# Talking-heads attention and FFN: scores per head with full-height query blocks, moved by SBUF-to-SBUF DMA into tiles of 10 queries x 12 heads for head mixing; q and k transposed by DMA

## The chip, the cores and the metric

The kernel runs on one core of one Trainium2 chip. The metric is the device time of one execution, in microseconds; the text gives medians. Before the change it was 792.39 us (3 runs, 792.29 to 793.1).

## The reference

Eight batches, 12 heads, 448 positions, head dimension 64; inputs and output are float32. The heads are mixed twice, by two 12 x 12 matrices, before and after the softmax. Then comes a feed-forward layer (FFN) with squared ReLU.

```python
# q, k, v: (8, 12, 448, 64); w_pre, w_post: (12, 12)
scores = scale * np.matmul(q, k.transpose(0, 1, 3, 2))
scores = np.einsum('bhij,hg->bgij', scores, w_pre)       # mix heads
attn = softmax(scores)                                    # over j
attn = np.einsum('bhij,hg->bgij', attn, w_post)          # mix heads
out = np.matmul(attn, v)                                  # -> x, (3584, 768)
h = np.maximum(x @ w_in, 0.0)                             # w_in: (768, 2048)
return h * h @ w_out                                      # w_out: (2048, 768)
```

## The kernel before

TensorE works in the program's order. All other engines' instructions are ordered by a scheduler when the kernel is built. Each engine then runs its own queue strictly in order; the timelines below show VectorE doing so, with 10.4 us idle before one copy and ready work behind it.

To mix heads, heads must lie on partitions. The kernel before gets this from score matmuls of 32 columns: 16 queries of two heads at a time, four row and column tiles of the array in parallel. Twelve heads x 16 queries are 192 rows, so that two chunks of 16 queries fill three tiles of 128 partitions, and the mixing matmuls need several matrices (`preA`, `preBA`, `preBB`) and two passes. q and k are transposed by TensorE, as units of the batch before.

```python
    def transposes(ps, tiles, p):                 # q and k: TensorE, 4 per pair of heads
        for st in range(4):
            n = ROWS[st]
            nc.tensor.transpose(ps[:, 128 * st:128 * st + n],
                                tiles[st][0:n, 2 * p:2 * p + 2, :].rearrange("s h d -> s (h d)"), ident[0:n, 0:n])

    def k_unit(b, p):
        ps = bank("kt_ps", BF16)
        transposes(ps, staged[b][1], p)
        ...
        nc.scalar.copy(out=kt_p[:, :], in_=ps[:, 0:S])
        ...
    # ... (q_unit: the same, evacuated by VectorE)

    def score_tile(s, t):
        b, c = s
        ps = bank("s_ps")
        for r in range(4):
            p, n = (r, 2 * c + t) if t < 2 else (4 + r % 2, 2 * c + r // 2)
            nc.tensor.matmul(ps[32 * r:32 * r + 32, 0:S], lhsT=ql[b % 2][p][:, n, :], rhs=kts[(b, p)][:, :],
                             start=True, stop=True)
        ...

    def mix_O(s, u):
        ps = bank("m_ps")
        nc.tensor.matmul(ps[:, 0:S], lhsT=preA[:, 0:128], rhs=S_sb[(s, u)][:, :], start=True, stop=False)
        nc.tensor.matmul(ps[:, 0:S], lhsT=preBA[u][:, :], rhs=S_sb[(s, 2)][:, :], start=False, stop=True)
        softmax_tile(s, ps, u)
    # ... (mix_AB, mix_BB: the third tile; post, post_last: the second mixing)
```

The softmax here doesn't subtract the row's maximum and nothing guards it: scores larger than these inputs give would overflow.

## Time and profile before

| | before |
|---|---|
| time, median | 792.39 us |
| TensorE (PE) busy | 750.2 us, 95% |
| VectorE (DVE) / ScalarE (ACT) busy | 62% / 61% |
| first mixing matmul at | 27.9 us |
| start to start of the batches | 67.5 us (no FFN in it), then 93 to 95, the last 84.1 |
| after the last mixing matmul | 48.5 us |

The batch times are read from the starts of the mixing matmuls in the trace. The head of the profile page shows the busy time of each engine with its share and number of instructions; a row of 40 digits shows the granted TensorE clock in tenths (9 is full speed); the queue lines give packets, MB and the share of the 16 DMA engines' time; the chain is the work that ended last, by engine.

```profile
span 791.2 us, 18851 instructions
PE 750.2 (95%) x7586; PEld 428.6 (54%) x7586; DVE 488.6 (62%) x1249; ACT 482.3 (61%) x1337; POOL 243.2 (31%) x271
...
PEclk9999999999999999999999999999999999999999
...
q0 software_dynamic: 140032, 23.60, 39.0%
q1 hardware_dynamic: 8704, 11.03, 4.2%
...
PE 85%; DVE 11%; DMA 2%; ACT 1%; issue 1%; ACTq 0%; DVEq 0%
```

TensorE is the limit: it is busy nearly all the time, at full clock, and 85% of the chain lies on it. The list of waits (what waited <- what released it: us in total, times, longest) shows that it hardly waits:

```profile
PE at_ps L359 <- DVE d_sb L315: 20.3, 29, 3.4
PE kt_ps L180 <- DMA kst<-in_k_dram: 10.1, 4, 6.0
```

### The profile page before, as it was taken

The numbers are of one execution on the slowest core, as the hardware profiler recorded it, in microseconds if no ns is written. First come the engines' busy times: TensorE is split into PE (matmuls) and PEld (weight loads), VectorE is DVE, ScalarE is ACT, GpSimd is POOL, SyncE is SP. The second block draws the span as 40 slices with busy tenths as digits, with TensorE's granted clock in tenths as the row PEclk, the third lists the DMA queues.
The fourth block names the chain that finished last, engine by engine and source line by source line (L and its number), as shares of the span: only waits on it lengthen the run. The fifth ranks groups of instructions, "written<-read, shape, count | busy, mean of one in ns | idle before, by whom it ended". The sixth has DMA issues, their size and how long they took to land.

```text
span 791.2 us, 18851 instructions
## 1 busy us (share of the span) xinstructions
PE 750.2 (95%) x7586; PEld 428.6 (54%) x7586; DVE 488.6 (62%) x1249; ACT 482.3 (61%) x1337; POOL 243.2 (31%) x271
## 2 busy tenths in 40 slices
PE   3689899999999999999999999999999999999997
PEld 1245455555555555556555555555555565555654
DVE  2889868557685577656676576855766556555500
ACT  1477767547664577556766466754776457664641
POOL 6835255200570023700445005620053000420070
PEclk9999999999999999999999999999999999999999
DMA  9999967310690124911637106731060010001002
GB/s 111 74 206 158 66 41 51 42 46 7 41 72 31 41 16 28 70 42 31 41 25 57 51 12 41 50 42 46 7 42 1 32 41 2 2 12 50 12 1 70
DMA packets 149336, 35.85 MB, mean 45 GB/s; under 512 B 139264, under 2 KB 148480, under 8 KB 149248
## 3 DMA queue, kind: packets, MB, share of 16 engines
q0 software_dynamic: 140032, 23.60, 39.0%
q1 hardware_dynamic: 8704, 11.03, 4.2%
q8 instruction: 59, 0.97, 0.5%
q14 instruction: 29, 0.24, 0.1%
q10 hardware_dynamic: 512, 0.01, 0.1%
HBM read 47.21 MB, written 11.01 MB: 74 GB/s over the span
## 4 chain that ended last, share of the span: by engine, by line
PE 85%; DVE 11%; DMA 2%; ACT 1%; issue 1%; ACTq 0%; DVEq 0%
PE o_ps L263 19%; PE h_ps L245 18%; PE s_ps L291 8%; PE m_ps L327 6%; PE at_ps L345 6%; DVE d_sb L315 6%; PE at_ps L348 5%; PE m_ps L328 5%; PE mB_ps L321 4%; PE ot_ps L223 4%; DVE at L350 3%; PE mB_ps L305 2%; PE qt_ps L180 2%; PE kt_ps L180 2%; PE at_ps L359 2%; DMA postB_col<-in_w_post_dram 1%
## 5 line engine op out<-in xcount | busy, mean ns | idle before, releaser
L350 DVE CAST at<-at_ps 128x384 bf16<-128x384 f32 x336 | 184.0, 552 | 93.3 <-PE at_ps L348 90.4
L315 DVE TENSOR_SCALAR d_sb<-e_sb,rc 128x448 bf16<-128x448 f32 x336 | 171.9, 514 | 7.6
L295 ACT CAST s_sb<-s_ps 128x448 bf16<-128x448 f32 x224 | 108.2, 535 | 54.7 <-PE s_ps L291 52.8
L311 ACT ACTIVATE e_sb<-m_ps 128x448 f32<-128x448 f32 x224 | 121.1, 545 | 27.8 <-issue 23.9
L249 ACT ACTIVATE hr<-h_ps 128x448 f32<-128x448 f32 x128 | 69.7, 544 | 84.8 <-PE h_ps L245 84.0
L313 DVE RECIPROCAL rc<-sm 128x1 f32<-128x1 f32 x336 | 53.6, 160 | 100.5 <-ACT e_sb L311 99.6
L348 PE MATMUL at_ps<-postA,d_sb 128*128 128x192 bf16 x672 | 110.3, 246 | 0.0
L345 PE MATMUL at_ps<-postBB,d_sb 128*128 128x384 bf16 x336 | 109.9, 327 | 0.0
L297 DVE CAST s_sb<-s_ps 128x448 bf16<-128x448 f32 x112 | 69.8, 623 | 40.9 <-PE s_ps L291 40.9
L348 PEld LDWEIGHTS <-d_sb 128*128 128x128 bf16 x672 | 65.7, 98 | 40.8 <-issue 0.2
L327 PE MATMUL m_ps<-s_sb,preA 128*128 128x448 bf16 x224 | 80.3, 358 | 0.0
L269 ACT COPY osb<-o_ps 128x384 f32<-128x384 f32 x56 | 26.8, 479 | 71.4 <-PE o_ps L263 61.0
L311 ACT ACTIVATE e_sb<-mB_ps 128x448 f32<-128x448 f32 x112 | 63.1, 563 | 8.4 <-PE mB_ps L321 6.6
L359 PE MATMUL at_ps<-postA,d_sb 128*32 128x192 bf16 x448 | 37.3, 249 | 20.9 <-DVE d_sb L315 20.3
L82 POOL DMA_DIRECT2D v_0_79<-in_v_dram x4 | 4.3, 1066 | 152.0 <-PE ot_ps L230 151.2
L71 POOL DMA_DIRECT2D kst<-in_k_dram x32 | 32.1, 1012 | 51.9 <-PE kt_ps L180 43.6
L236 ACT ACTIVATE xt<-ot_ps,bvec 128x224 bf16<-128x224 f32 x96 | 37.7, 444 | 14.6 <-PE ot_ps L230 13.9
L311 ACT ACTIVATION_READ_ACCUMULATOR e_sb<-m_ps 128x1 f32 x224 | 46.1, 206 | 0.0
L245 PE MATMUL h_ps<-xt,w_0_191 128*128 128x448 bf16 x128 | 45.1, 353 | 0.0
L245 PE MATMUL h_ps<-xt,w_5_196 128*128 128x448 bf16 x128 | 45.1, 353 | 0.0
L245 PE MATMUL h_ps<-xt,w_2_193 128*128 128x448 bf16 x128 | 45.1, 352 | 0.0
L245 PE MATMUL h_ps<-xt,w_3_194 128*128 128x448 bf16 x128 | 45.1, 352 | 0.0
(602 smaller groups left out, 1921.4 us busy)
## 6 DMA issues: line engine op xcount, KB each, us to landing
out_dram<-osb SPq DMA_DIRECT2D x48, 192.0 KB, 1.9
kst<-in_k_dram POOLq DMA_DIRECT2D x24, 192.0 KB, 5.2
qst<-in_q_dram POOLq DMA_DIRECT2D x24, 192.0 KB, 5.0
out_dram<-osb SPq DMA_DIRECT2D x16, 96.0 KB, 2.2
kst<-in_k_dram POOLq DMA_DIRECT2D x8, 96.0 KB, 4.6
qst<-in_q_dram POOLq DMA_DIRECT2D x8, 96.0 KB, 3.9
v_0_76<-in_v_dram POOLq DMA_DIRECT2D x4, 192.0 KB, 4.7
v_1_77<-in_v_dram POOLq DMA_DIRECT2D x4, 192.0 KB, 6.0
```

The source lines that it names most:

```text
L245: nc.tensor.matmul(ps[:, 0:S], lhsT=w1[c2][:, ft * 128:(ft + 1) * 128], rhs=xts[(b, c2)][:, :], start=(c2 == 0), stop=(c2 == NPAIR - 1))
L249: nc.scalar.activation(out=hr[:, :], in_=ps[:, 0:S], func=ACT.Relu)
L263: nc.tensor.matmul(dst, lhsT=h2ts[(b, ft)][:, mt * 128:mt * 128 + ROWS[mt]], rhs=w2[ft][:, n2 * 384:(n2 + 1) * 384], start=(ft == 0), stop ...
L291: nc.tensor.matmul(ps[32 * r:32 * r + 32, 0:S], lhsT=ql[b % 2][p][:, n, :], rhs=kts[(b, p)][:, :], start=True, stop=True)
L295: nc.scalar.copy(out=sb[:, :], in_=ps[:, 0:S])
L297: nc.vector.tensor_copy(out=sb[:, :], in_=ps[:, 0:S])
L311: nc.scalar.activation(out=e[:, :], in_=ps[:, 0:S], func=ACT.Exp, scale=SCALE, accum_out=sm[:, 0:1])
L315: nc.vector.tensor_scalar(out=d[:, :], in0=e[:, :], scalar1=rc[:, 0:1], scalar2=1.0 / S, op0=ALU.mult, op1=ALU.subtract)
L327: nc.tensor.matmul(ps[:, 0:S], lhsT=preA[:, 0:128], rhs=S_sb[(s, u)][:, :], start=True, stop=False)
L345: nc.tensor.matmul(ps[:, 0:384], lhsT=D_sb[(s, 2)][:, js], rhs=postBB[:, :], start=True, stop=False, skip_group_check=True)
L348: nc.tensor.matmul(ps[:, 192 * u:192 * u + 192], lhsT=D_sb[(s, u)][:, js], rhs=postA, start=False, stop=True, skip_group_check=True)
L350: nc.vector.tensor_copy(out=at[:, jb, :, CH * cc:CH * cc + CH].rearrange("p g (u i) -> p g u i", u=2), in_=ps[:, 0:384].rearrange("p (u g ...
```

## The change

The intent is to take work from TensorE. Scores are computed per head for a block of 120 queries at a time (a full-height tile, two heads side by side in the rows of the array). A DMA within SBUF, the gather, then takes 10 queries x 12 heads out of the score tile onto 120 partitions, so that each tile is mixed by one matmul with one block matrix. q and k are no longer transposed by TensorE. They are loaded in runs of 1 KB into `raw`, put in order by a copy on VectorE into `rows` (one buffer), and transposed from there by four DMA transposes each, on the same in-order SyncE (SP) queue as the gathers.

```diff
-    def transposes(ps, tiles, p):
-        ... nc.tensor.transpose(...)
+    def load_raw(src, b, name):
+        t = work.tile([PR, H, NR, D], BF16, name="raw", tag="raw", bufs=2)
+        nc.gpsimd.dma_start(out=t[:, :, :, :], in_=src[b].rearrange("h (p r) d -> p h r d", r=NR))
+        return t
+    def turn(raw, dst):
+        t = work.tile([PR, NR, H, D], BF16, name="rows", tag="rows", bufs=1)
+        nc.vector.tensor_copy(out=t[:, :, :, :].rearrange("p r h d -> p h r d"), in_=raw[:, :, :, :])
+        for r in range(NR):
+            nc.sync.dma_start_transpose(out=dst[:, :, PR * r:PR * r + PR],
+                                        in_=t[:, r, :, :].rearrange("p h d -> p (h d)"))
-    def score_tile(s, t): ...
+    def scores(b, t, c):
+        ...
+                nc.tensor.matmul(ps[:, hh, 0:S], lhsT=qt[x][r, p, BQ * t:BQ * t + 128], rhs=kt[x][r, p, :], ...)
+        ...
-    def mix_AB(s), mix_BB(s), mix_O(s, u): ...
+    def gather(b, t, m):
+        n = min(TQ, BLOCKS[t] - TQ * m)
+        sx = work.tile([P, S], BF16, name="sx", tag="sx", bufs=8)
+        nc.sync.dma_start(out=sx[0:H * n, :], in_=sqs[(b, t)][TQ * m:TQ * m + n, :, :])
+        return sx, H * n
+    def pre(s):
+        ...
+            nc.tensor.matmul(ps[:, y, 0:S], lhsT=pre_w[0:rows, :], rhs=sx[0:rows, :], start=True, stop=True)
+        ...
+    # per batch 23 steps of two tiles; the turn of the next batch's k at step 7, of its q at step 9,
+    # load of the next v at step 8; gathers run 6 tiles ahead (AHEAD = 6)
 ... (second mixing, attention x V, output store: same idea, other shapes)
```

## The prediction

> **What bounds it now.** TensorE. The table of engines gives PE 95% of 791 us, DVE 62%, ACT 61%, POOL 31%; the chain of waits lies 85% on PE. Busy time overstates it, so I count start-to-start in the timeline: a 448-column matmul starts every 0.187 us, a 384-column one every 0.16, 192 columns 0.08; four 32-column score matmuls share one 0.19 slot; an attention-times-V pair of 112 columns takes 0.05; matmuls with 128-column weights and one moving column start every 25 ns, so weight loads are hidden. By batch that sums to FFN 35.8 us, scores+mixing+post 39, attention times V 4.5, q/k transposes about 5, bias 1.3: 86 us. The batch period in the timeline is 93.8; the rest is gaps (about 0.1 us at changes of array tiling, some waits for d_sb).
>
> **What the change does to PE, per batch (estimates from these intervals).** Scores: 24 pairs of row-tiled matmuls at 0.187 = 4.5 us (was 7.8). Pre-mix: 45 tiles x 0.187 = 8.4 (was 15.7). Post: 180 matmuls of 120 columns x 0.053 = 9.5 (was 15.7). Attention times V: 96 pairs x 0.052 = 5. Transposes 5 and bias 1.3 vanish. FFN stays 35.8. Total 63, with tiling changes about 67 us instead of 86. So PE gives up about 19-23 us per batch, 150-180 us in all, and all of that was on the critical path.
>
> **What takes over.** DVE, per batch, scaled from measured 0.62 us (448 columns out of PSUM), 0.55 (384), 0.51 (d_sb), 0.16 (reciprocal): post evictions of 960 columns 23 x 1.15 = 26; d 45 x 0.5 = 23; score evictions 8 x 1.1 = 9; reciprocals 4; xt now on DVE 4.5; the two reorder copies 2-6. Sum 69, about 62 after instruction overlap. ACT: exp 45 x 0.65, score evictions 16 x 0.85, relu and output: about 53. PSUM is now three two-bank pairs plus two banks; 70 pair uses of roughly 2.6 us per batch fill the pairs for about 60 us. Everything is thus near 60-67 us and coupled in order, so I expect 75-85 us per batch, not 67: PE will wait for pair banks (DVE eviction of at_ps, exp).
>
> **DMA.** Loads get cheaper (1 KB runs instead of 256 B; the software queue falls from 140,032 packets to under 50,000). New: 360 SBUF-to-SBUF gathers of 107 KB in 896 B packets. The Trainium skill, "DMA: Bandwidth & Descriptors", on why a DMA increments its semaphore by 16, says the engine count divides both outer sizes: here 10 of 16. "SBUF — State Buffer", Door 1, gives 27 GB/s per port with four neighbouring partitions on one port: ten source partitions, hence up to 1.6 us per gather (estimate; nothing here shows it yet). I expect 3-5 us to landing, covered by the six-tile lead (about 10 us). The 64 DMA transposes share the in-order SP queue; four of them in a row, at a guess 6-8 us, may just delay gathers once or twice per batch.
>
> **Sum.** Start-up about 34 us (transposes and first gather lengthen it slightly), batch 0 without FFN 70, seven batches at 80, tail of unhidden FFN 42: 706 us.
>
> Prediction: **705 us**, 650 to 785 in 8 of 10. Faster by over 2%: 0.83; within 2%: 0.07; slower: 0.10.
>
> **Right if:** PE busy falls to 590-650 us; DVE rises to 65-80% of the span; PE's largest waits are for pair banks freed by DVE or ACT; waits for sx at most 30 us in total; the last 40 us are FFN as before.
>
> **Wrong if:** waits for sx (gathers) or for kt/qt (DMA transposes) dominate: transposes above 5 us each block SP and, through the single rows buffer, DVE; then 800 or more. Or row-tiled score pairs do not overlap (+36 us). Or batches run at 67-70 us because the pairs suffice: 640.

## The result, and the profile after

The changed kernel took 843.73 us in the median (837.96 to 846.7, 4 runs) against 792.34 (792.01 to 793.1, 4 runs) of the kernel before: a ratio of 1.064, with a 95% interval of 1.058 to 1.070. It is slower. Ratios here are the mean time of one kernel's fast runs over that of the other's of the same rounds, so not quite the ratio of the medians.

The same lines of the page, of the changed kernel, with the large loads in place of the chain (KB each, us from issue to landing):

```profile
span 842.3 us, 14918 instructions
PE 626.4 (74%) x5514; PEld 358.1 (43%) x5514; DVE 486.0 (58%) x895; ACT 406.7 (48%) x1033; POOL 166.1 (20%) x193
...
PEclk9999965599888999689977999769997999799999
...
q1 hardware_dynamic: 100738, 60.59, 38.8%
q0 software_dynamic: 35840, 22.81, 20.8%
...
raw<-in_k_dram POOLq DMA_DIRECT2D x8, 672.0 KB, 9.4
raw<-in_q_dram POOLq DMA_DIRECT2D x8, 672.0 KB, 10.1
v_67<-in_v_dram POOLq DMA_DIRECT2D x4, 672.0 KB, 7.7
```

TensorE's busy time fell by 124 us, as intended, and no engine took its place: VectorE is less busy in share than before. The kernel waits. TensorE's waits, changed kernel:

```profile
PE m_ps L274 <- DMA sx<-sq: 71.3, 40, 18.8
PE s_ps L249 <- DMA qt_69<-rows: 38.4, 1, 38.4
PE at_ps L300 <- ACT e L277: 23.3, 36, 0.9
PE at_ps L300 <- DVE sq L254: 17.3, 6, 9.5
PE ot_ps L175 <- DVE xt L182: 17.1, 7, 10.3
PE s_ps L249 <- DVE at_108 L305: 14.3, 5, 8.4
```

One wait of 38.4 us for q's transposes stands at the start. Of the 71.3 us for gathers, 36.5 lie in the first 110 us. The rest is spread over releases by VectorE, with single waits of 8 to 10 us: much longer than anything VectorE computes. What VectorE itself waited for is in its groups (columns: count | busy us, mean ns | idle just before, and what ended most of it):

```profile
L274 PE MATMUL m_ps<-sx,pre_w 120*128 120x448 bf16 x360 | 120.8, 405 | 79.4 <-DMA sx<-sq 71.3
...
L81 DVE COPY rows<-raw 112x3072 bf16<-112x3072 bf16 x16 | 15.4, 960 | 117.6 <-DMA qt_69<-rows 37.4
```

The 16 copies into `rows` take 15.4 us and VectorE stands idle for 117.6 us before them. Of these, 102.2 us end when transposes release the buffer, 38.6 of them in the first 110 us; VectorE's waits:

```profile
DVE rows L81 <- DMA qt_69<-rows: 37.4, 3, 16.9
DVE rows L81 <- DMA kt_71<-rows: 24.8, 3, 13.5
DVE rows L81 <- DMA qt_70<-rows: 21.6, 2, 11.2
DVE rows L81 <- DMA kt_72<-rows: 18.4, 3, 8.2
```

Start to start of the batches, against before (batch 7 is counted to its last mixing matmul, so it is not a full period):

| | start | batch 0 | 1 | 2 | 3 | 4 | 5 | 6 | 7 | tail |
|---|---|---|---|---|---|---|---|---|---|---|
| before | 27.9 | 67.5 | 93.8 | 94.8 | 93.3 | 93.9 | 93.9 | 93.6 | 84.1 | 48.5 |
| after | 60.6 | 93.8 | 100.3 | 99.7 | 96.6 | 97.1 | 87.0 | 81.6 | 76.9 | 48.7 |

The loss of 51 us is made of 33 at the start, 26 in batch 0, and nothing gained in batches 1 to 6 taken together (1 us), with 7 gained in the last. Batches 6 and 7 run at 82 and 77 us. What sets them apart from batches 1 to 5 is that no transposes are left to do, and no copies and no loads of q and k (the scheduler places the transposes about 15 steps earlier than the program has them, and the last ones, for batch 7, were issued at 601 to 623 us, in batch 5).

Step by step the place is exact. Each batch has 23 steps; these are the times in us from the first mixing matmul of a step to that of the next, worked out from the trace:

| after, step | 17 | 18 | 19 | 20 | 21 | 22 |
|---|---|---|---|---|---|---|
| batch 2 | 3.4 | 3.6 | 6.8 | 17.2 | 7.1 | 1.8 |
| batch 3 | 2.1 | 4.0 | 9.3 | 14.7 | 6.5 | 2.2 |
| batch 4 | 3.4 | 3.6 | 9.8 | 13.5 | 7.6 | 1.7 |
| batch 6 | 3.4 | 3.6 | 4.0 | 5.2 | 5.5 | 2.2 |

Steps 0 to 18 of batches 2 to 5 are on average longer than those of batch 6 by 0.6 us in sum. Steps 19 and 20 are longer by 4.5 and 7.5 us. Batch 5 tells something by itself: it still has eight transposes, but behind the last four no copy and no raw load follows. Its step 20 takes 5.1 us, no longer than in batch 6. The timeline of VectorE over these two steps of batch 3 (start, duration, operation, in brackets idle before and its releaser):

```profile
414.92 1.15 DVE L305 CAST at_110<-at_ps 112x960 bf16<-112x960 f32 x1
421.17 0.96 DVE L81 COPY rows<-raw 112x3072 bf16<-112x3072 bf16 x1 [5.10 <-DMA kt_72<-rows]
422.05 0.16 DVE L280 RECIPROCAL rc<-sm 120x2 f32<-120x2 f32 x1
...
425.96 1.15 DVE L305 CAST at_110<-at_ps 112x960 bf16<-112x960 f32 x1
437.50 0.96 DVE L81 COPY rows<-raw 112x3072 bf16<-112x3072 bf16 x1 [10.39 <-DMA qt_70<-rows]
438.38 0.16 DVE L280 RECIPROCAL rc<-sm 120x2 f32<-120x2 f32 x1
```

The first copy (q) waits for the four transposes of k out of the only `rows` buffer; the second (the next batch's k, whose transposes come 65 us later) waits for the four of q. Reciprocals, `d` and evictions that are ready stand behind it in the in-order queue. Those four transposes, on SyncE's queue (durations of the issue, min/median/max ns):

```profile
L83 SPq DMA_TRANSPOSE qt_70<-rows x4: 1371/2324/3755, 424.0 to 432.5; - x4
```

They were issued at 424.0, 425.4, 429.2 and 432.5 and landed 10.2, 10.8, 7.6 and 4.9 us after that. In the same time a 672 KB load of the next raw q, which the first copy had let go at 422.4, was on the DMA engines; it landed at 434.4. The busy time in the stretches around it (columns: us, busy us of PE, PEld, DVE, ACT, POOL, granted clock, DMA share, GB/s):

```profile
390.00:416.00 26.00, 24.85 (x224) 14.66 (x222) 19.73 (x35) 16.79 (x45) 6.04 (x6) 1.00 0.51 92
416.00:421.00 5.00, 4.40 (x33) 2.38 (x33) 0.07 (x1) 2.88 (x6) 0.00 (x0) 1.00 0.73 134
421.00:427.00 6.00, 2.83 (x15) 1.64 (x15) 5.76 (x10) 1.54 (x3) 1.18 (x1) 0.73 0.76 121
427.00:438.00 11.00, 3.62 (x46) 2.45 (x45) 0.61 (x2) 1.59 (x5) 0.00 (x0) 0.81 1.40 141
438.00:450.00 12.00, 8.59 (x87) 5.16 (x86) 6.95 (x13) 3.46 (x9) 1.18 (x1) 0.74 0.58 83
```

Up to 416 us TensorE is busy 24.85 of 26 us at full clock. In the 11 us of the second hold it is busy 3.6 and its clock is cut; the clock is still at 0.74 in the 12 us after it. (A DMA share above 1 is as the view gives it; it is not used here.) The Trainium skill, "TensorE: Matmul & The Clock Gate", Part 1, says that the clock falls to half after an idle window of about 3.4 us. The trace agrees in kind: its clock records hold 1.0 and 0.5 alone, and the mean is 0.893 against 0.997 before, low where TensorE had waited. We read it as a consequence of the stalls that lengthens them; no run tests it apart.

At the start the same picture is larger. The four transposes of the first q, issued from 24.0 us, landed 5.1, 13.1, 23.0 and 31.3 us after issue, among the loads of the next raw tiles and the FFN weights, which were issued from 25 us on.

### The profile page after: what moved, and what is told of

Its sections match the earlier page's. It is cut to its first block, busy times and chain, and to the rows that moved or that the text cites. A ratio compares the mean times of both kernels' runs of the same rounds, so it can differ in the third digit from the quotient of the medians.

```text
span 842.3 us, 14918 instructions
## 1 busy us (share of the span) xinstructions
PE 626.4 (74%) x5514; PEld 358.1 (43%) x5514; DVE 486.0 (58%) x895; ACT 406.7 (48%) x1033; POOL 166.1 (20%) x193
## 5 line engine op out<-in xcount | busy, mean ns | idle before, releaser
L277 ACT ACTIVATE e<-m_ps 120x448 f32<-120x448 f32 x360 | 192.7, 541 | 246.5 <-issue 117.9
L274 PE MATMUL m_ps<-sx,pre_w 120*128 120x448 bf16 x360 | 120.8, 405 | 79.4 <-DMA sx<-sq 71.3
L252 ACT CAST sq<-s_ps 128x896 bf16<-128x896 f32 x128 | 112.9, 910 | 55.8 <-PE s_ps L249 55.6
L280 DVE RECIPROCAL rc<-sm 120x2 f32<-120x2 f32 (+1 forms) x184 | 29.5, 161 | 102.5 <-ACT e L277 101.6
L254 DVE CAST sq<-s_ps 128x896 bf16<-128x896 f32 x64 | 69.5, 1086 | 26.8 <-PE s_ps L249 24.8
L81 DVE COPY rows<-raw 112x3072 bf16<-112x3072 bf16 x16 | 15.4, 960 | 117.6 <-DMA qt_69<-rows 37.4
L305 DVE CAST at_109<-at_ps 112x960 bf16<-112x960 f32 (+1 forms) x63 | 71.0, 1128 | 14.2 <-PE at_ps L300 14.1
L305 DVE CAST at_108<-at_ps 112x960 bf16<-112x960 f32 (+1 forms) x63 | 71.0, 1127 | 13.5 <-PE at_ps L300 13.5
L249 PE MATMUL s_ps<-kt_71,qt_69 64*128 64x448 bf16 x192 | 36.1, 438 | 55.0 <-DMA qt_69<-rows 38.4
L305 DVE CAST at_110<-at_ps 112x960 bf16<-112x960 f32 (+1 forms) x58 | 65.8, 1135 | 15.2 <-PE at_ps L300 15.2
L277 ACT ACTIVATION_READ_ACCUMULATOR e<-m_ps 120x1 f32 x360 | 72.3, 201 | 0.0
L274 PEld LDWEIGHTS <-pre_w 120*128 120x128 bf16 x360 | 32.0, 105 | 78.9 <-DMA sx<-sq 55.2
L189 PE MATMUL h_ps<-xt,w_0_116 128*128 128x448 bf16 x128 | 46.8, 366 | 0.0
L189 PE MATMUL h_ps<-xt,w_1_117 128*128 128x448 bf16 x128 | 46.4, 363 | 0.0
L189 PE MATMUL h_ps<-xt,w_2_118 128*128 128x448 bf16 x128 | 46.0, 360 | 0.0
L189 PE MATMUL h_ps<-xt,w_5_121 128*128 128x448 bf16 x128 | 45.7, 357 | 0.0
L189 PE MATMUL h_ps<-xt,w_4_120 128*128 128x448 bf16 x128 | 45.7, 357 | 0.0
L189 PE MATMUL h_ps<-xt,w_3_119 128*128 128x448 bf16 x128 | 45.6, 356 | 0.0
L249 PE MATMUL s_ps<-kt_72,qt_70 64*128 64x448 bf16 x192 | 33.3, 406 | 10.4 <-DVE at_108 L305 5.1
```

Of the source, the lines that this page charges most:

```text
L81: nc.vector.tensor_copy(out=t[:, :, :, :].rearrange("p r h d -> p h r d"), in_=raw[:, :, :, :])
L189: nc.tensor.matmul(ps[:, 0:S], lhsT=w1[c2][:, ft * 128:(ft + 1) * 128], rhs=xts[b][:, c2, :], start=(c2 == 0), stop=(c2 == NPAIR - 1))
L249: nc.tensor.matmul(ps[:, hh, 0:S], lhsT=qt[x][r, p, BQ * t:BQ * t + 128], rhs=kt[x][r, p, :], start=True, stop=True)
L252: nc.scalar.copy(out=sq[:, 2 * p:2 * p + 2, :], in_=ps[:, :, 0:S])
L254: nc.vector.tensor_copy(out=sq[:, 2 * p:2 * p + 2, :], in_=ps[:, :, 0:S])
L274: nc.tensor.matmul(ps[:, y, 0:S], lhsT=pre_w[0:rows, :], rhs=sx[0:rows, :], start=True, stop=True)
```

## The experiments

All have the edit stated against the changed kernel ("after"), or against another experiment where said. Steps, batches and waits are read as above.

| run | median us | ratio to before | start | batches 1-6, mean |
|---|---|---|---|---|
| after | 843.7 | 1.064 | 60.6 | 93.7 |
| e1_two_rows | 853.5 | 1.076 | 68.5 | 93.1 |
| e2_weights_later | 852.4 | 1.075 | 41.7 | 93.6 |
| e3_pe_transposes | 754.0 | 0.952 | 28.8 | 85.6 |
| e4_transposes_on_act | 846.1 | 1.067 | 52.9 | 94.0 |
| e5_transposes_unused | 855.9 | 1.079 | 41.1 | 93.4 |
| e6_copies_on_gpsimd | 844.0 | 1.064 | 44.1 | 94.7 |
| e7_first_batch_by_pe | 829.0 | 1.046 | 28.8 | 93.4 |
| e8_longer_lead | 750.6 | 0.946 | 28.9 | 85.5 |
| e9_program_order | 823.1 | 1.037 | 60.9 | 90.9 |
| e10_order_and_first_pe | 806.3 | 1.017 | 32.9 | 90.9 |
| e11_dve_order_only | 838.4 | 1.058 | 58.9 | 94.0 |
| e12_lead_and_order | 779.8 | 0.982 | 28.4 | 88.6 |
| e13_rows_loaded_direct | 805.1 | 1.015 | 36.7 | 91.1 |
| e14_direct_and_first_pe | 797.1 | 1.006 | 35.1 | 90.5 |
| e15_unused_in_order | 818.7 | 1.033 | 29.8 | 92.2 |
| e16_pe_order_control | 759.1 | 0.957 | 32.9 | 85.7 |
| e17_v_load_later | 783.8 | 0.990 | 34.6 | 88.4 |
| e18_spread_transposes | 800.5 | 1.008 | 34.0 | 91.7 |

### First round: which part of the change costs

**e1_two_rows.** Two `rows` buffers, so that a copy need not wait for the transposes before it. SBUF is full, so one `raw` buffer had to go for it.

```diff
-        t = work.tile([PR, H, NR, D], BF16, name="raw", tag="raw", bufs=2)
+        t = work.tile([PR, H, NR, D], BF16, name="raw", tag="raw", bufs=1)
-        t = work.tile([PR, NR, H, D], BF16, name="rows", tag="rows", bufs=1)
+        t = work.tile([PR, NR, H, D], BF16, name="rows", tag="rows", bufs=2)
```

> The changed kernel with two rows buffers and one raw buffer instead of one and two (same memory; all DMA transposes stay on the same queue, in the same number). Theory H (hold): the slow batches are slow because VectorE, in order, is held by the reorder copy that waits until the four DMA transposes have left the single rows buffer (5 and 11 us per batch in the trace). Then the waits of rows for kt/qt transposes fall from 116 us to under 40 (start-up only), the batch period of batches 1 to 5 falls from 97-100 us to 78-84, and the time falls by 60 to 90 us, to 755-785 us. Theory Q (queue): the gathers come late because SP issues transposes and stores in order ahead of them; then the periods stay at 95-100 us and the time stays within 15 us of 844.

Measured: 853.45 us (850.93 to 854.18). The hold did not go, it changed its cause; waits of VectorE:

```profile
DVE rows L81 <- DMA raw<-in_q_dram: 60.4, 7, 16.8
...
DVE rows L81 <- DMA kt<-rows: 25.6, 5, 6.3
DVE rows L81 <- DMA raw<-in_k_dram: 20.1, 2, 12.7
```

With one `raw` buffer the load of q starts only when the copy of k is done, and VectorE stands at the second copy for that load. This run could not separate the theories, and it shows why: it took one wait away and made another in the same place.

**e2_weights_later.** The 22 loads of FFN weights spread over the first steps, each behind a one-element GpSimd write that depends on that step.

```diff
+    def paced_load(d):
+        t, src = wloads.pop(0)
+        nc.gpsimd.tensor_copy(out=t[0:1, 0:1], in_=d[0:1, 0:1])
+        nc.gpsimd.dma_start(out=t[:, :], in_=src)
     ... (called once per step, while loads are left)
```

> The changed kernel with the 22 FFN weight loads tied one by one to the first 22 steps instead of being issued at 25-66 us. Theory L (loads): start-up (first mixing matmul at 60.6 us against 27.9 before) and batch 0 (94 us against 67) are long because the transposes and the first gathers share the DMA engines with the weight loads. Then the first mixing matmul comes at 35-45 us, batch 0 takes 70-80 us, and the time falls by 25 to 45 us, to 800-820. Rival: the transposes and gathers are slow by themselves; then the start moves by less than 8 us and the time stays within 10 us of 844. The later batches stay at 97-100 us under both.

Measured: 852.42 us (846.73 to 857.53). The first mixing matmul came 19 us earlier (41.7), so the weights had been in the way of the first transposes; but batch 0 took 117.1 instead of 93.8 us. In total this run is 9 us slower than the changed kernel.

**e3_pe_transposes.** q and k transposed by TensorE straight from `raw`, evacuated by ScalarE and VectorE; no copies, no DMA transposes. Everything else of the change stays.

```diff
-    def turn(raw, dst): ... tensor_copy ... 4 x nc.sync.dma_start_transpose ...
+    def turn_unit(raw, dst, p, eng):
+        ps = bankp.tile([P, 1024], BF16, name="t_ps", tag="bank")
+        for r in range(NR):
+            for hh in range(2):
+                nc.tensor.transpose(ps[64 * hh:64 * hh + 64, PR * r:PR * r + PR], raw[:, 2 * p + hh, r, :],
+                                    ident[0:PR, 0:PR])
+        (evacuate to dst[:, p, 0:S]: k by ScalarE, q by VectorE)
     ... (12 units for the next batch, one per step from step 8)
```

> The changed kernel with q and k transposed by TensorE again, straight from raw (no reorder copies, no DMA transposes, everything else of the change kept). Theory H: no VectorE hold is left; PE gains about 5 us per batch; batch periods 80-87 us, start-up shorter by 10-20 us (first mixing matmul at 40-50 us), the time 745-780. If instead the gathers themselves set the pace (theory G), the periods stay above 92 us and waits for sx grow, time above 810.

Measured: 754.02 us (753.11 to 756.25), 4.8% faster than before and 90 us faster than the changed kernel. Start 28.8 us; batches 84.3 to 87.1, the last 76.1. So the score blocks, the gathers and the one-matmul mixing do pay, even with TensorE doing the transposes. The whole loss is in the way q and k are transposed. TensorE's waits for gathers fell from 71.3 us to:

```profile
PE m_ps L291 <- DMA sx<-sq: 48.0, 40, 7.2
```

**e4_transposes_on_act.** The DMA transposes issued by ScalarE instead of SyncE.

```diff
-            nc.sync.dma_start_transpose(
+            nc.scalar.dma_start_transpose(
```

> The changed kernel with the 64 DMA transposes issued from the ScalarE queue instead of SP; the single rows buffer stays. Theory Q: SP is free for gathers, waits of the mixing matmul for sx fall below 40 us and the time falls by 30 us or more. Theory H: the transposes still hold the rows buffer, VectorE still waits 80 us or more for them, and ScalarE loses 64 issues of 1.3 us or more; the time stays within 20 us of 844 or gets longer.

Measured: 846.05 us (844.74 to 848.77). SyncE's queue is not the sole place of the cost. The stall moved with the issue: step 18 of batches 2 to 5 took 13 to 18 us (batch 6: 3.6), and steps 19 and 20, where the changed kernel stalls, were normal. The Trainium skill, "DMA: Bandwidth & Descriptors", Issuing engines are not separate DMA queues, says that issuing on several engines only saves the issuing sequencer's time. The run agrees, and ScalarE's queue paid with its own work: TensorE's waits for ScalarE's `e` at `at_ps` rose from 23.3 to 64.1 us.

### Second round: hold or load

Two theories were left. *Hold*: transposes cost because somebody waits for them at the head of an in-order queue. *Load*: they cost by occupying SyncE's queue and the DMA engines, whoever waits.

**e5_transposes_unused.** e3, with 64 DMA transposes beside it whose result nobody reads.

```diff
+    def idle_turn(raw):
+        for r in range(NR):
+            nc.sync.dma_start_transpose(out=idle_t[:, :, PR * r:PR * r + PR],
+                                        in_=raw[:, 3 * r:3 * r + 3, :, :].rearrange("p h r d -> p (h r d)"))
     ... (k at step 7, q at step 9, as in after)
```

> The kernel of the third experiment (q and k transposed by TensorE, 754.0 us), and beside it the same number of DMA transposes as in the changed kernel, 64 of 112 x 768, issued by SyncE at the same steps from the loaded rows into a scratch tile that nobody reads. No engine waits for their result and VectorE makes no copies for them. Theory L (load): the DMA transposes cost by what they put on SyncE's queue and on the DMA engines; gathers behind them come late. Then most of the 90 us between 754 and 844 returns: 810 us or more, waits of TensorE for sx 80 us or more, a period of 92 us or more in batches 1 to 5. Theory H (hold): they cost because somebody waits for them: VectorE, held in its in-order queue at a copy that waits for the previous four transposes, and TensorE for kt and qt at the start. Then 754 to 770 us and a period of 85 to 87. Start-up (first mixing matmul at 28.8 us without them) tells the same apart: L 45 us or more, H 35 or less.

Measured: 855.86 us (854.33 to 858.17): all of the loss is back, with no copy and no reader. That looked like the load theory. The trace of it says otherwise in part; waits of SyncE's own queue:

```profile
SPq L98 <- DMA raw<-in_k_dram: 45.2, 7, 8.4
```

The scheduler had put each group of eight transposes before a block's first gathers, where SyncE waited up to 8.4 us for the load of k. The stall is one step per batch (step 22, 11 to 13 us instead of 2.2) and in batch 0 one step of 41.9 us. So a hold had come back, on SyncE. e15 repeats this without it.

**e6_copies_on_gpsimd.** The copies into `rows` on GpSimd, in program order there.

```diff
-        nc.vector.tensor_copy(out=t[:, :, :, :].rearrange("p r h d -> p h r d"), in_=raw[:, :, :, :])
+        nc.gpsimd.tensor_copy(out=t[:, :, :, :].rearrange("p r h d -> p h r d"), in_=raw[:, :, :, :])
```

> The changed kernel with the copies into rows on GpSimd, in program order there, so that VectorE never waits for a DMA transpose or a load; transposes, gathers and buffers as they were. Theory H: VectorE's waits of about 110 us in all for kt and qt vanish, batches 1 to 5 fall from 97-100 us to 87-90, the total to 780-800; start-up stays at 50-60 us or grows a little, as a GpSimd copy is slower than the one on VectorE. Theory L: the same transposes load the same queue, so 835-850 and a period of 96 or more.

Measured: 843.99 us (838.87 to 849.33). VectorE waited for no transpose any more, and nothing was won. (A copy took 2.74 us on GpSimd, against 0.96 on VectorE.) The stall is now step 11 (13 to 14 us in batches 2 to 6), and the waits of SyncE's queue name the new place:

```profile
SPq L83 <- POOL h L194: 75.7, 12, 11.6
...
SPq L83 <- POOL rows L81: 17.8, 3, 9.7
```

SyncE stands at q's transposes until GpSimd has come to the copy. The gathers of the next block stand behind it: in batch 3 none was issued between 351.7 and 375.9 us. The expectation had overlooked that GpSimd's queue holds SyncE's.

**e7_first_batch_by_pe.** Only batch 0 by TensorE.

```diff
-        turn(raws.pop(("k", 0)), kt[0])
-        turn(raws.pop(("q", 0)), qt[0])
+        for _, f in turn_units(0):
+            f()
```

> The changed kernel with q and k of batch 0 alone transposed by TensorE; batches 1 to 7 go through copies and DMA transposes as in the changed kernel. It measures the start-up by itself. If start-up and steady batches are separate costs, the first mixing matmul moves from 60.6 us to 29-32, batch 0 stays at 94 or a bit less, later batches stay at 97-100, and the total is 805-815 us. If the late start is hidden by something later (weights that arrive no sooner, as in the second experiment, where 19 us saved at the start came back as 23 us in batch 0), the total stays above 825.

Measured: 829.01 us (827.06 to 830.92). The start moved from 60.6 to 28.8 us, but batch 0 grew to 110.6: one wait of 21.5 us of TensorE was for VectorE, held at the copy for batch 1. Half of the late start had hidden this. 15 us are the start's own.

**e8_longer_lead.** e3 with a lead of 10 gathers and 12 `sx` buffers (the room of `rows`).

```diff
-    AHEAD = 6       # sx bufs=8
+    AHEAD = 10      # sx bufs=12
```

> The kernel of the third experiment (754.0 us) with a lead of 10 gathered tiles and 12 sx buffers instead of 6 and 8; the space is that of the rows tile that it does without. It is a try for a faster version and a test of whether the gathers still bound it. If its 48 us of TensorE waits for sx are from too short a lead: they fall to 20 us or less, a batch from 85 to 81-83 us, the total to 725-740. If the waits come at block changes, where gathers can't start before the scores are evacuated whatever the lead: 745-756, waits for sx 35 us or more.

Measured: 750.64 us (748.8 to 753.21), the fastest kernel, 5.4% faster than before. TensorE's waits for `sx` stayed at 47.5 us, so they don't come from a short lead. That fits the second alternative (a block's gathers can't start before its scores are evacuated), and the trace bears it out: 35.9 of the 47.5 us stand at the first step of a block. 25.9 of the 47.5 us are in batch 0.

### Third round: the order of the queues

**e9_program_order, e10_order_and_first_pe, e11_dve_order_only, e12_lead_and_order.** If queues are held because the scheduler puts a waiting copy ahead of ready work, the program's order (copy of k at step 7, of q at step 9) should mend it. e10 is e7 with the same edit, e11 has VectorE alone, e12 is e8 with the edit, as a control without DMA transposes.

```diff
-    with tc.manual_schedule(engines={PE}):
+    with tc.manual_schedule(engines={PE, DVE, SP, Pool}):     # e9, e10, e12
+    with tc.manual_schedule(engines={PE, DVE}):               # e11
```

> The changed kernel, every instruction as it was, with VectorE, SyncE and GpSimd issuing in the program's order (as TensorE does already) instead of the order that the scheduler chose. So the copy of the next k is no longer placed 20 steps early, ahead of work that is ready, where it waits for the last four transposes; the copy for q comes two steps after the one for k; and the four transposes of each stand in SyncE's queue behind the gathers of their own step. Theory O (order): the transposes are cheap by themselves (2.7 us to landing when nothing else runs) and what costs about 15 us a batch is that a wait for them stands at the head of some in-order queue, VectorE's in the changed kernel, ScalarE's, SyncE's or GpSimd's in the experiments so far. Then the two stalls of a batch (steps 19 and 20: 5 and 10 us) vanish, batches 1 to 5 run in 81-85 us instead of 97-100, VectorE's waits for kt and qt fall below 20 us, start-up stays at 50-60 us, and the total is 765-790. Theory L (load): the transposes cost through SyncE's queue and the DMA engines whatever the order: a stall of 10 us or more stays somewhere in each batch, a period of 93 or more, 830 us or more.

> Both mends at once: program order as in the ninth experiment, and q and k of batch 0 by TensorE as in the seventh. If the start and the hold are the two costs of the change and are separate, about 30 us less than the ninth experiment: 735-760, the first mixing matmul at 29-32 us, batch 0 at 82-90 us. It may beat the kernel with TensorE transposes throughout (754.0 us), as TensorE and both evacuating engines have less to do per batch. If load counts, 800 or more.

> As the ninth experiment with VectorE alone in program order, SyncE and GpSimd in the scheduler's. Theory O says that every in-order queue counts: VectorE's waits for kt and qt vanish; whether SyncE now holds the gathers behind transposes that wait for their copy is open. If VectorE's hold was all: within 1% of the ninth experiment. If SyncE then holds: a stall of 8 us or more per batch stays, with TensorE's waits for sx above 100 us, 820 or more. Theory L: 830 or more for both.

> The kernel of the eighth experiment (TensorE transposes, lead of 10 tiles, 750.6 us), with VectorE, SyncE and GpSimd in program order. A control: it has no DMA transposes, so no queue is held by them, and the order should matter little: 740-758 us. If program order by itself were worth much, apart from the transposes, it would show here as 735 or less, and the ninth experiment would have to be read with that gain taken off.

Measured: 823.12, 806.30, 838.44 and 779.77 us. e9 gained 21 us on the changed kernel, less than expected, and e10 another 17, far from its 735 to 760. The stall did get smaller and moved to step 9, the copy of q: 6.7 to 14.4 us there, where batch 7 without transposes needs 4.8. The control explains part of the miss: program order cost it 29 us, so that e9 had to pay for that as well. Read against their controls, the copies and DMA transposes cost 90 us in the scheduler's order (after against e3) and 43 us in program order (e9 against e12, which also has the longer lead). In e11, with VectorE alone in order, step 9 takes 13 to 15 us in batches 2 to 5, 9 to 10 us too long: the copy of q, two steps after the one of k, waits for k's transposes there (55.9 us in 7 waits, which were expected to vanish).

### Fourth round: no holds, same transposes

**e13_rows_loaded_direct, e14_direct_and_first_pe.** q and k loaded directly in the order that the transposes read (runs of 256 bytes in DRAM, four loads each, three buffers), so that there is no copy at all. SyncE and GpSimd in program order, VectorE not. e14 also has batch 0 by TensorE.

```diff
-        t = work.tile([PR, H, NR, D], BF16, name="raw", tag="raw", bufs=2)
-        nc.gpsimd.dma_start(out=t[:, :, :, :], in_=src[b].rearrange("h (p r) d -> p h r d", r=NR))
+        t = work.tile([PR, NR, H, D], BF16, name="rows", tag="rows", bufs=3)
+        for r in range(NR):
+            nc.gpsimd.dma_start(out=t[:, r, :, :], in_=src[b].rearrange("h (p r) d -> p r h d", r=NR)[:, r, :, :])
 ...
-        t = work.tile([PR, NR, H, D], BF16, name="rows", tag="rows", bufs=1)
-        nc.vector.tensor_copy(out=t[:, :, :, :].rearrange("p r h d -> p h r d"), in_=raw[:, :, :, :])
 ...
+    with tc.manual_schedule(engines={PE, SP, Pool}):
```

> The changed kernel without the copies on VectorE: q and k are loaded in the order that the transposes read, in runs of 256 bytes, four loads each, into three buffers (the space of the two raw buffers and the rows tile); SyncE and GpSimd issue in program order, VectorE in the scheduler's as in the changed kernel. All 64 DMA transposes stay, on SyncE, at the same steps; their loads were asked for seven steps (25 us) earlier. No engine but SyncE can be held. Theory O (a wait at the head of an in-order queue): no stall of 5 us or more in a batch other than what the batches without transposes have, period 81-85 in batches 1 to 5, total 755-785, with the late start (45-60 us) left in it. Theory L (load of the transposes): a stall of 8 us or more near steps 8 to 11, period 92 or more, 815 us or more.

> As the thirteenth, with q and k of batch 0 transposed by TensorE (four transposes per pair of heads, as the loaded order allows). Under O: the first mixing matmul at 28-32 us, batches as in the thirteenth, total 725-755, which may be the fastest of all. Under L: 785 or more.

**e15_unused_in_order, e16_pe_order_control.** e5 and e3 with SyncE and GpSimd in program order.

```diff
-    with tc.manual_schedule(engines={PE}):
+    with tc.manual_schedule(engines={PE, SP, Pool}):
```

> The fifth experiment again (TensorE transposes, and 64 DMA transposes that nobody reads; it took 855.9 us, and its trace shows SyncE held before each group by a load that hadn't landed), now with SyncE and GpSimd in program order, so that the loads have landed seven steps before. Same transposes, same queue, same count. Under O: within 15 us of its control, the sixteenth experiment, and no stall of 8 us in a batch. Under L: 60 us or more above the control.

> The kernel of the third experiment (754.0 us) with SyncE and GpSimd in program order: the control for the thirteenth and the fifteenth. The twelfth, which had VectorE in program order too, was 29 us slower than its own counterpart; if that came from VectorE, this one is at 745-765; if from SyncE or GpSimd, at 775-785.

Measured: e13 805.12, e14 797.10, e15 818.70, e16 759.14 us. Neither theory holds alone. e13 is 39 us faster than the changed kernel, all 64 transposes kept, and in batches 1 to 6 no step is longer than 7.6 us. But e15 is 60 us slower than its control, with transposes that nobody reads and, after batch 0, loads that had landed long before. (At the first groups SyncE still stood 7.1 and 6.7 us, once each. Of the 56 us between the two profiled executions, 17 are in start and batch 0, and 39, or 6.5 each, in batches 1 to 6.) e16 shows that the order of SyncE and GpSimd costs only 5 us with the shorter lead, so that most of the 29 us of e12 came from VectorE's order.

What is left in e13 lies in steps 10 to 12, which take 17 to 20 us where e16 takes 10 to 13. TensorE's waits for gathers, first e16, then e15:

```profile
PE m_ps L291 <- DMA sx<-sq: 52.2, 38, 11.0
```

```profile
PE m_ps L298 <- DMA sx<-sq: 93.7, 58, 17.1
```

In e13's trace, batch 4, k's four transposes and then q's four, as SyncE issued them (two windows of the same line, min/median/max ns):

```profile
L82 SPq DMA_TRANSPOSE kt<-rows x4: 1222/1230/2529, 428.9 to 434.2; - x4
```

```profile
L82 SPq DMA_TRANSPOSE qt<-rows x4: 1843/2548/2964, 439.4 to 447.4; - x4
```

k's transposes, but for the first, took 1.23 us to issue and 2.6 us to land. q's took 1.8 to 3.0 us to issue, and the first two landed after 8.8 us. Between them the 672 KB load of v had been asked for (step 8; issued 436.3, landed 447.6); the first q transpose landed 0.6 us after it. Three gathers before them took 6.3 to 9.1 us to land instead of 3.6 to 4.4.

### Fifth round: what a transpose meets on its way

**e17_v_load_later, e18_spread_transposes.** e14 with the load of v at step 14; then also one transpose per step in steps 5 to 12.

```diff
-                if in_b == 8 and b + 1 < B:
+                if in_b == 14 and b + 1 < B:
                     load_v(b + 1)
 ... e18 in addition:
-                if in_b == 7 ...: turn(k of b + 1)      # four in a row
-                if in_b == 9 ...: turn(q of b + 1)
+                if 5 <= in_b < 13 and b + 1 < B:
+                    n = "k" if in_b < 9 else "q"
+                    turn(raws[(n, b + 1)], (kt if n == "k" else qt)[(b + 1) % 2], ((in_b - 5) % 4,))
```

> The fourteenth kernel (797.1 us) with the load of v for the next batch asked for at step 14 instead of step 8, so that it no longer shares the DMA engines with the transposes of q (steps 9 and 10). Nothing else differs. Theory C (collision with a large load): q's transposes issue in about 1.25 us and land in 2.7-4 us like k's, the excess at steps 10 to 12 falls from about 9 us a batch to 4 or less, batches 1 to 6 from 90.5 to 85-87, total 760-775. Theory I (issue time): eight transposes at 1.25 us keep SyncE from gathers for 10 us within three steps whatever else is in flight: 785-800, excess 7 us or more.

> As the seventeenth, with the eight DMA transposes of a batch issued one per step in steps 5 to 12 instead of four at step 7 and four at step 9. SyncE has about 1.5 us to spare in a step of 3.6 us with two gathers of 0.83 us, and the lead of six tiles stays. If what is left is issue time in one lump, the rest of the excess goes: a period of 82-84 us in batches 1 to 6, 740-757 us in all, level with or faster than TensorE transposes (750.6 us with the longer lead). If spreading gains nothing beyond the seventeenth, within 1% of it, the transposes disturb the gathers in flight rather than hold SyncE.

Measured: e17 783.76 us (781.06 to 790.92), 13 us better than e14, between the two expected ranges for collision (760 to 775) and bare issue time (785 to 800). e18 800.48 us: spreading made it worse, against the expectation. The issue times show one reason. First e17, four transposes of q in a row and the last three of k; then e18, four of k, one per step:

```profile
L86 SPq DMA_TRANSPOSE qt<-rows x4: 1230/1230/1915, 421.9 to 426.5; - x4
L86 SPq DMA_TRANSPOSE kt<-rows x3: 1226/1230/1231, 414.1 to 416.7; - x3
```

```profile
L86 SPq DMA_TRANSPOSE kt<-rows x4: 2105/2324/2507, 420.4 to 432.8; - x4
```

A transpose that has only other transposes just before it issues in 1.23 us. In e18 every transpose follows two gathers, and issues in 2.26 us (median of the 48 after the first 130 us). In all these 48 its first piece landed just after the gather before it had landed entirely: 0.59 us later in the median, 0.55 to 0.62 from the tenth to the ninetieth percentile. So the transpose seems to wait for the transfers in flight, and SyncE is kept for a part of that time: its issue is longer by about 1 us and ends 1.4 us (median) before that gather has landed. In a row, only the first of four pays this. Spreading them paid it eight times: about 18 us of SyncE's time per batch (8 x 2.26, an estimate from these medians) instead of some 12 (two firsts at 2.2, six at 1.23). The loss itself shows later. Steps 10 to 13 together are no longer in e18 (16 to 19 us) than in e17 (18 to 20), but steps 15 and 16 together take 9 to 14 us where e17 takes 7 to 8. There the load of v and eight loads for the next batch are on the DMA engines in both kernels, and in batches 3, 5 and 6 gathers there take up to 8 us (e17) and 11 us (e18) to land. That SyncE comes to this point in e18 with its lead used up is the likely reading; it was not tested.

## Why the prediction was wrong

**Right: what TensorE gives up.** Busy 626 us, predicted 590 to 650. (The prediction also says 150 to 180 us given up; busy time fell by 124, at a mean granted clock of 0.893 instead of 0.997.) The row-tiled score pairs overlap (4 ns between starts in the median), and the second mixing's matmuls start every 0.053 us, as costed.

**Right in number, partly by luck: a batch without transposes.** Predicted 75 to 85, most likely 80, for every batch; batch 6 of the changed kernel, without transposes, ran in 82. The reason given was waits for pair banks on top of 67 us of TensorE work. In batch 6 TensorE was busy for 72.9 of 81.6 us at a mean granted clock of 0.94, and all its waits come to 8.8 us, those for ScalarE's `e` to 3.2 and those for gathers to 3.8: TensorE itself, and not the pair banks, fills such a batch. The tail was FFN as before, 48.7 us (predicted 42).

**Right: the gather by itself.** Predicted 3 to 5 us to landing; measured 4.0 in the median, on 10 of 16 engines. The engine count is what the Trainium skill says in "DMA: Bandwidth & Descriptors", Why a DMA increments its semaphore by 16 and not by 1, and the semaphore records agree (8 engines for the last tile of a batch). The prediction's estimate of up to 1.6 us for the transfer fits too: the packets of a gather that found no transfer in flight span 1.7 us (median of 12). Whether the ports or the ten engines set this is not shown.

**Wrong, the step that failed:** "The 64 DMA transposes share the in-order SP queue; four of them in a row, at a guess 6-8 us, may just delay gathers once or twice per batch." The prediction costed the transposes as a short delay, and the copies as 2 to 6 us of VectorE's work per batch. It put down nothing for the time in which a queue stands at a copy that waits for transposes. Measured: VectorE worked 15.4 us on copies and stood 117.6 us before them, 102.2 of these for transposes. The 6 to 8 us for four in a row hold only undisturbed (6.6 us for the last four of the kernel, from the first issue to the last landing); the groups for batches 3 to 7 before them took 9 to 16 us. Its own last paragraph names this case ("through the single rows buffer, DVE; then 800 or more"), but all that could make the kernel slower had a chance of 0.10 together, and this is what came: 843.7 us. Replacing only this part (e3) gives 754.0, so this step carries 90 of the 139 us between prediction and result. Of the other 49, 14 are in batch 0 of e3 (84.3 instead of 70), 7 in the tail, and most of the rest in batches 1 to 6 (85.6 instead of 80), where TensorE does the transposes again.

**Where those 90 us are**, as a path of runs, each a measured kernel:

| from | to | us |
|---|---|---|
| after, 843.7 | e13: no copies, rows loaded direct, no queue but SyncE can be held | -38.6 |
| e13, 805.1 | e14: batch 0 by TensorE | -8.0 |
| e14, 797.1 | e17: v's load not among the transposes | -13.3 |
| e17, 783.8 | e16: no DMA transposes | -24.6 |
| e16, 759.1 | e3: scheduler's order for SyncE and GpSimd | -5.1 |

The order of such a path is a choice, and e13, e14 and e17 spread over 7 to 10 us each, so that its smaller lines are rough. The first line is the hold, together with the other load pattern that was needed to take it away and with the program order of SyncE and GpSimd; the path does not separate these. That the hold is the stall in the changed kernel is seen directly in the timeline (in batch 3 VectorE idles 5.1 and 10.4 us, in two steps that are 5.3 and 9.5 us longer than in batch 6), and e4, e5, e6 show the stall following the wait to ScalarE's, SyncE's and GpSimd's queue. The third is the collision with a large load. The fourth is what is left of seven batches' DMA transposes with nobody else held (the loads differ too between these two kernels, and v's load is back at step 8 in e16): SyncE's issue time and what the transfers do to each other. e18 shows one mechanism in it; how it divides is open.

**Wrong: the start.** "Transposes and first gather lengthen it slightly", 34 us; it was 60.6. The first q transposes landed 5 to 31 us after issue among the weight loads. e2 (weights later) brought the start to 41.7, which supports that, but neither e2 nor e7 kept the gain whole: of 19 and 32 us nothing and 15 were left.

**Wrong: what would limit.** The prediction put pair banks freed by VectorE and ScalarE first and waits for `sx` at most at 30 us. The waits for `sx` were 71.3 us (46.0 of them in batch 0), with 38.4 for q at the start, and VectorE was at 58%, not 65 to 80. (Its 486 us of work are as predicted, 62 us per batch; the span was longer.) Even in e3 the waits for `sx` are 48.0 us: a second, smaller mis-sizing, of the gathers at block changes, above all in batch 0, which has 28.5 of them (e8: a longer lead doesn't help).

**What remains open.** Why VectorE's program order costs 29 us (e12 against e8) was not tested. The traces give a hint of the same kind: VectorE's idle time before reciprocals that wait for ScalarE's `e` is 185.2 us in e12 and 110.5 in e8. A DMA-transposing version that beats TensorE transposes was not found; e17 at 783.8 is the best one, 1% faster than before. The fastest is e8.

## What to carry to other kernels

Cost a wait at the place where it stands in an in-order queue, not only the work that ends it: a 1 us copy that waits 10 us for a DMA holds everything behind it, and moving it to another engine moves the hold. Giving a TensorE-bound kernel's transposes to the DMA is no gift when the DMA queue already feeds TensorE: here some TensorE time per batch in e3 was much cheaper than eight DMA transposes. When one part of a large change is suspected, put back just that part first: one run (e3) found the 90 us, and the other seventeen only explain them.

## What the Trainium skill lacked or had wrong

- "DMA: Bandwidth & Descriptors", DMA Transpose (X-bar): no time for a transpose of this size and none for its issue, alone or beside other transfers (the same page gives an effective bandwidth elsewhere, and "VectorE: DVE Perf Modes" a time for 128 x 128). For 112 x 768 bf16 from SBUF to SBUF: 1.23 us to issue and 2.6 to 2.7 to landing with only other transposes in flight; 2.26 and 4.45 behind two gathers (e18); 9 us beside a 672 KB load (e13); up to 31.3 us among the weight loads at the start.
- The same page, Rules for kernel authors, has "A transpose next to ordinary DMAs needs nothing". For correctness that agrees (all runs were correct). For time it lacks that a transpose's first piece landed 0.59 us (median) after the gather in flight before it, never earlier (48 of 48 in e18), and that its issue then took 2.26 us instead of 1.23.
- The same page, Issuing engines are not separate DMA queues, calls the sequencer's time "usually small relative to the DMA itself". Here a gather takes 0.83 us of 4.0 and a transpose 1.23 of 2.7 in the issuing queue, and moving the transposes to ScalarE (e4) gained nothing.
- "Advanced Engine Details and Errata", X-Bar Transpose (TRN2): "TRN2 transpose DMAs are as fast as regular DMAs". A transpose alone (168 KB, 2.6 us) is no slower than a gather (105 KB, at least 3.6 us), so it agrees alone, not among other transfers.
- "VectorE: DVE Perf Modes", Rules for kernel authors, advises TensorE for a transpose if a PSUM destination will do. The runs agree (754.0 against 843.7 us); the page gives no reason beyond the time of one transpose.
- "TensorE: Matmul & The Clock Gate" calls the queues of ScalarE and VectorE strictly first in, first out (engine queue depths), and the traces agree. No page was found on what a wait at the head of such a queue costs; here 117.6 us of VectorE's idle time before 15.4 us of copies.
